# Counts of six expert searches from two tiles of tokens a matmul, with left sides of 128 columns

## The chip, the cores and the metric

One core of one Trainium2 chip runs the whole kernel as one program. The metric is the device time of one execution in microseconds (us); the time before is the median of three runs. The engines have the names of the profile: PE (TensorE's matmuls), PEld (its weight loads), DVE (VectorE), ACT (ScalarE), POOL (GpSimd) and SP (which issues most DMAs).

## The reference, cut to what matters

Three stages follow one another: attention over pooled keys and values, a layer of eight experts with a greedy assignment of tokens, and a two-layer MLP.

```python
def reference(**kwargs):
    attn_out = _attn_ref(**attn_kwargs)            # (8, 8, 576, 64)
    x = ascontiguousarray(attn_out.transpose(0, 2, 1, 3)).reshape(4608, 512)
    x = _moe_ref(x=x, **moe_kwargs)
    return _moe2_ref(x=x, **moe2_kwargs)           # h = x @ w_in; (h - tanh(h)) @ w_out

def _moe_ref(x, w_gate, w1, w2):                   # N = 4608 tokens, E = 8, F = 1024
    cap = N // E
    logits = x @ w_gate
    order = np.argsort(-logits.flatten())
    for idx in order:                              # largest logit first, over all tokens and experts
        tok, e = (int(idx) // E, int(idx) % E)
        if assigned[tok] >= 0 or counts[e] >= cap:
            continue
        assigned[tok] = e
        counts[e] += 1
    for e in range(E):
        mask = assigned == e
        h = np.maximum(x[mask] @ w1[e], 0.0)
        out[mask] = h @ w2[e]
```

An expert takes a token until it has 576 of them; then it is closed, and the tokens left over go to their next best open expert.

## The kernel before, in words

Tokens stand in 36 tiles of 128 (`NT = 36`), a token a partition. The greedy loop is replaced by a search: for the experts in the order in which they fill up (k = 0 to 7), the kernel finds the logit at which the next expert reaches 576 tokens (`fast_search` for k = 0, `search` for k = 1 to 6; k = 7 takes the rest without a search), closes that expert (`fill`), turns its tokens into a list of rows (`route_rows`) and gathers them (`gather`).

A search of k = 1 to 6 has two parts of three steps. In a step, DVE compares the key of each token with 40 to 42 thresholds and writes the ones and zeros as `at` [128, 36, n], n being the number of thresholds. `count` then adds over the tokens: for each tile j a matmul has `self.ohb[:, j, :]` on the left (128 tokens by 8, a one at the token's best expert) and `at[:, j, :]` on the right, and all 36 add up in `p2` [8, n] in PSUM: for each expert, how many of its tokens lie at or above each threshold. DVE compares `p2` with what each expert still lacks (`ok`, in a tile named `pass`, so it stands as `pass` in the profile), one matmul with ones (`pass,ones` in the profile) adds this over the experts for all partitions, and DVE makes the next threshold from it (`jm`). So a step is a chain: at on DVE, the count on PE, pass on DVE, a matmul on PE, jm on DVE. For k = 1 `at` and the count go in three pieces of 8, 12 and 16 tiles; for k = 2 to 6 DVE writes all 36 tiles in one instruction and the 36 matmuls are one unit for the planner (line 662; the matmuls that the planner places one by one stand on line 131). The search of k = 0 has six steps with 17 or 19 thresholds and three pieces.

`route_rows` builds two matrices of ones and zeros for each tile, `oa` (40 columns, the left side) and `ob` (32 columns), and adds `oa.T @ ob` over the 36 tiles in a PSUM tile `pp` named `tr`; `sp` and five matmuls with `sel5` (`sp,sel` in the profile) spread it.

An expert's products are 384 matmuls with 128 by 128 on the left and 288 columns on the right, in fp32r, split into high and low parts (`mm<-parts` and `m<-parts` in the profile).

The order on each engine is not written out by hand. `Plan` records every operation with an estimated cost, and `placed` puts the operations one after another, the most urgent first, into the earliest gap on their engine, where a reader on PE also gets a margin after its inputs: 0 for the routing of k = 1, 0.2 us for k = 2, 0.8 us for k from 3. The routing of expert k has an urgency so that it runs beside the products of experts k - 2 and k - 1. Each engine then executes its list in order.

The names and lines that matter: `count` (657), `fast_search` (681), `search` (762), `route_rows` (926), `Recorder` (131, the line on which every operation placed one by one is shown).

Of the kernel before, what the change touches and what calls it, by code (L numbers as in the profile page):

```python
# [9 lines left out]
F32 = mybir.dt.float32  # L10
F32R = mybir.dt.float32r
BF = mybir.dt.bfloat16
# [3 lines left out]
AF = mybir.ActivationFunctionType  # L16
OP = mybir.AluOpType
# [7 lines left out]
NT = N // 128  # L25
# [9 lines left out]
RADIX = 41  # L35
# [244 lines left out]
class Kernel:  # L280
# [25 lines left out]
    def route_consts(self, tp):  # L306
# [46 lines left out]
        nc.vector.tensor_scalar(t("w8c", [128, 1], F32), pef, -1.0, 8.0, op0=OP.mult, op1=OP.add)  # L353

        for nm, shape, dt in (("pass", [128, 18], F16), (f"pass{RADIX - 1}", [128, RADIX], F16),
                              (f"pass{RADIX}", [128, RADIX + 1], F16), ("dl", [128, 8], F16), ("sp", [128, 32], BF)):
            nc.vector.memset(t(nm, shape, dt), 0.0)
            if nm[:4] == "pass":
                nc.vector.memset(c[nm][:8, shape[1] - 1:], 1.0)
# [247 lines left out]
    def best(self, js=slice(0, NT), first=False):  # L607
# [19 lines left out]
        V.tensor_tensor(sg, mi, sg, op=OP.bitwise_xor)  # L627
        self.ohb = rp.tile([128, NT, 8], BF, name="ohb")
        V.tensor_tensor(self.ohb[:, js], oh, bc(mw), op=OP.is_equal)
# [26 lines left out]

    def count(self, out, at, js, whole=False):

        if whole:
            def products():  # L660
                for j in js:
                    last = self.nc.tensor.matmul(out, self.ohb[:, j, :], at[:, j, :], start=j == 0, stop=j == NT - 1)  # L662
                return last

            self.plan.call("tensor", products, [self.ohb, at], [out], 0.026 * len(js) + 0.18)
            return
        for j in js:
            self.plan.tensor.matmul(out, self.ohb[:, j, :], at[:, j, :], start=j == 0, stop=j == NT - 1)

# [14 lines left out]
    def fast_search(self, hl):  # L684
# [15 lines left out]
        for i in range(6):  # L700
# [4 lines left out]
            for a, b in ((0, 8), (8, 20), (20, NT)):  # L705
                x = v[:, a:b, None].to_broadcast([128, b - a, n])
                y = c["th"][:, i, None, :n].to_broadcast([128, b - a, n])
                if t is None:
                    V.tensor_tensor(at[:, a:b], x, y, op=OP.is_ge)
                else:  # L710
                    V.scalar_tensor_tensor(at[:, a:b], x, t, y, op0=OP.subtract, op1=OP.is_ge)
                self.count(p2, at, range(a, b))
            if i == 0:
# [43 lines left out]
    def search(self, k, hl):  # L757
# [5 lines left out]
        for part in range(2):  # L763
            t = None
            for i in range(3):
# [5 lines left out]
                p2, p3 = bank[:8, :n], bank[:, 128:128 + n + 1]  # L771
                for a, b in ((0, 8), (8, 20), (20, NT)) if k == 1 else ((0, NT),):
                    x = v[:, a:b, None].to_broadcast([128, b - a, n])
                    y = th[:, None, :].to_broadcast([128, b - a, n])
                    if t is None:
                        V.tensor_tensor(at[:, a:b], x, y, op=OP.is_ge)
                    else:
                        V.scalar_tensor_tensor(at[:, a:b], x, t, y, op0=OP.subtract, op1=OP.is_ge)
                    self.count(p2, at, range(a, b), k > 1)
                if part and i == 0:  # L780
# [9 lines left out]
                if t is None:  # L790
                    ok = ok[:, :n]
                    inc = inc[:, :n]
                    p3 = p3[:, :n]
                V.tensor_scalar(ok[:8, :n], p2, lack, None, op0=OP.is_ge)
                nc.tensor.matmul(p3, c["ones"], ok, start=True, stop=True)
# [5 lines left out]
            y1, z1 = [rp.tile([8, RADIX], F32, name=nm) for nm in ("y1", "z1")]  # L801
            nc.scalar.activation(z1, p2, AF.Copy)
            nc.scalar.activation(y1, p3[:8, :n], AF.Copy)
# [5 lines left out]
        jn = rp.tile([8, RADIX + 1], F32, name="j8")  # L809
        V.tensor_scalar(jn, p2, lack, 0.0, op0=OP.is_ge, op1=OP.add, accum_out=ne)  # L810
        V.tensor_scalar(c["dl"][:8], c["blk"][:8], ne, None, op0=OP.mult)
        p4 = bank[:, 256:264]
        nc.tensor.matmul(p4, c["ones"], c["dl"], start=True, stop=True)
        y2 = rp.tile([8, RADIX + 1], F32, name="z2")
        nc.scalar.activation(y2, p2, AF.Copy)
        nm = rp.tile([128, 1], F32, name="nm")
# [110 lines left out]
    def route_rows(self, k, g):  # L927
# [11 lines left out]
        V.tensor_copy(gb, g2)  # L939
        oa = rp.tile([128, NT, 40], BF, name="oa")  # L940
        ob = rp.tile([128, 3, NT, 16], BF, name="ob")
        for j in range(0, NT, 12):
# [6 lines left out]
            else:  # L949
                nc.scalar.activation(ob[:, 1, js], ob[:, 2, js], AF.Copy, scale=c["pcol"])  # L950
            V.tensor_tensor(oa[:, js], bc(gb[:, 0, js], 40),
                            c["iota40"][:, None, :].to_broadcast([128, 12, 40]), op=OP.is_equal)
        pp = self.rps.tile([40, 32], F32, name="tr")
        for j in range(NT):
            nc.tensor.matmul(pp, oa[:, j, :], ob[:, 0:2, j, :], start=j == 0, stop=j == NT - 1)
        sp = c["sp"]
        V.tensor_copy(sp[:40], pp)
        pi = self.rps.tile([128, 5, 32], F32, name="tr")
# [93 lines left out]
    def products(self, nc, out, terms, first=True, last=True):  # L1052

        n = len(terms)
        for i, (wh, wl, xh, xl) in enumerate(terms):
            nc.tensor.matmul(out, wh, xh, start=first and i == 0, stop=False)
            nc.tensor.matmul(out, wh, xl, start=False, stop=False)
            nc.tensor.matmul(out, wl, xh, start=False, stop=last and i == n - 1)
# [411 lines left out]
```

## Time and profile before

| | us |
|---|---|
| median of three runs | 1487.55 (1486.27 to 1489.66) |
| profiled execution, its own time | 1487.64 |
| span of its core | 1485.9 |
| PE busy | 1441.4 (97%) |
| PEld busy | 1271.1 (86%) |
| DVE busy | 1190.2 (80%) |
| ACT busy | 809.2 (54%) |
| POOL busy | 318.2 (21%) |
| PE's share of the chain that ended last | 85% |

The execution has four stretches: attention until about 156 us, the routing of k = 0 until about 186 us, the experts with the routing of k = 1 to 7 beside their products until about 700 us, and the second MLP until the end. In the views, a row of the timeline gives the start of the first instruction of a group and the time until the end of its last; matmuls are pipelined, so a matmul's own duration (180 ns for one of the count) overlaps the next one's, and what a matmul costs its engine is read from start to start. A row's last bracket is the time the engine sat idle before it and what ended that.

### The profile page before, as it was taken

What the parts mean: (1) busy time and instruction counts of PE and PEld (TensorE: products, weight loads), DVE (VectorE), ACT (ScalarE), POOL (GpSimd) and SP (SyncE); (2) the same over time, 40 slices, a digit from 0 to 9 for tenths busy, and PEclk for the clock granted to TensorE, in tenths of its full rate; (3) what the DMA queues carried; (4) which work ended last, traced back from release to release, by engine and by line L of the source; (5) the groups of instructions that cost most, each with busy time, mean ns of one, the idle gap of its engine ahead of it and who ended that gap; (6) DMA issues with size and microseconds to landing.
All of it is one profiled execution on the core that took longest, in us unless ns stands there. A gap on an engine that the chain in (4) does not pass through costs nothing.

```text
span 1485.9 us, 25650 instructions
## 1 busy us (share of the span) xinstructions
PE 1441.4 (97%) x9763; PEld 1271.1 (86%) x9764; DVE 1190.2 (80%) x2506; ACT 809.2 (54%) x1463; POOL 318.2 (21%) x292
## 2 busy tenths in 40 slices
PE   8999599999999999999999999999999999999997
PEld 6999488999999999999788888888888888888885
DVE  8778878787899976875998787878878788787874
ACT  5444123335455576866665565655656565665653
POOL 5874101202224155553401010000101000010101
PEclk9999699999999999999999999999999999999999
DMA  9941124324525367665200010100001010000000
GB/s 385 373 175 74 52 67 137 108 67 144 185 86 189 102 190 252 232 212 159 71 30 29 1 57 1 37 21 29 29 1 57 1 36 22 29 29 1 29 1 28
DMA packets 98315, 138.51 MB, mean 93 GB/s; under 512 B 6928, under 2 KB 70416, under 8 KB 95504
## 3 DMA queue, kind: packets, MB, share of 16 engines
q1 hardware_dynamic: 87632, 108.04, 21.8%
q0 software_dynamic: 5952, 19.40, 3.7%
q10 hardware_dynamic: 4608, 9.44, 1.7%
q8 instruction: 76, 1.25, 0.4%
q14 instruction: 47, 0.39, 0.1%
HBM read 103.30 MB, written 33.55 MB: 92 GB/s over the span
## 4 chain that ended last, share of the span: by engine, by line
PE 85%; DVE 9%; issue 2%; DMA 2%; ACT 1%; POOL 1%; POOLq 0%; ACTq 0%; DVEq 0%; SPq 0%
PE mm L131 40%; PE m L131 19%; PE tr L131 8%; PE rt L131 7%; PE av L131 4%; PE sc L131 3%; PE pt L131 2%; DVE parts L131 2%; PE rt L662 2%; DVE g L131 2%; DVE ca L131 1%; DVE gl L131 1%; DMA xg<-xd,ix 1%; DVE oa L131 1%; DVE ob L131 0%
## 5 line engine op out<-in xcount | busy, mean ns | idle before, releaser
L131 PE MATMUL mm<-parts 128*128 128x288 f32 x2112 | 306.5, 300 | 2.0 <-DVE parts L131 2.0
L131 PEld LDWEIGHTS mm<-parts 128*128 128x128 f32 x2112 | 287.4, 189 | 4.8 <-DVE parts L131 2.2
L131 PE MATMUL mm<-parts,gh 128*128 128x512 f32 x792 | 244.0, 389 | 0.0
L131 DVE SCALAR_TENSOR_TENSOR g<-s,g 128x512 f32<-128x512 f32 x288 | 205.6, 714 | 2.8
L131 ACT ACTIVATE s<-u,pb 128x512 f32<-128x512 f32 x288 | 192.3, 724 | 0.0
L131 PEld LDWEIGHTS mm<-parts,gh 128*128 128x128 f32 x792 | 148.7, 188 | 30.8
L1319 POOL DMA_INDIRECT out<-y,ix x18 | 20.4, 1133 | 658.1 <-ACT y L131 637.4
L131 PE MATMUL mm<-parts,gl 128*128 128x512 f32 x396 | 154.4, 390 | 0.8 <-DVE gl L131 0.8
L131 PE MATMUL m<-parts 128*128 128x288 f32 x960 | 143.7, 302 | 0.1
L131 PE MATMUL m<-yh,parts 128*128 128x512 f32 x432 | 141.9, 389 | 0.0
L131 ACT ACTIVATE parts<-wr 128x512 fp32r<-128x512 f32 x148 | 90.9, 626 | 86.8 <-DMA wr<-w 32.7
L131 DVE TENSOR_TENSOR parts<-wr,parts 128x512 fp32r<-128x512 f32 x128 | 101.0, 804 | 42.1 <-ACT parts L131 41.7
L131 PEld LDWEIGHTS m<-parts 128*128 128x128 f32 x960 | 133.0, 191 | 1.1 <-DVE parts L131 0.2
L131 ACT ACTIVATE gh<-g 128x512 fp32r<-128x512 f32 x144 | 91.2, 633 | 74.0 <-DVE g L131 51.4
L131 DVE TENSOR_TENSOR gl<-g,gh 128x512 fp32r<-128x512 f32 x144 | 106.5, 740 | 21.1 <-ACT gh L131 21.1
L131 DVE COPY_PREDICATED g<-m,t 128x512 f32<-128x512 uint32 x144 | 109.5, 761 | 5.0
L131 ACT ACTIVATE u<-m 128x512 f32<-128x512 f32 x72 | 42.9, 596 | 116.2 <-PE m L131 116.2
L131 PEld LDWEIGHTS m<-yh,parts 128*128 128x128 f32 x432 | 81.1, 188 | 16.8
L131 DVE TENSOR_TENSOR g<-m,u 128x512 f32<-128x512 f32 x72 | 49.6, 688 | 54.5 <-ACT t L131 53.4
L131 PEld LDWEIGHTS mm<-parts,gl 128*128 128x128 f32 x396 | 74.4, 188 | 17.1 <-DVE gl L131 1.7
L131 PE MATMUL m<-yl,parts 128*128 128x512 f32 x216 | 84.1, 389 | 0.0
L131 PE MATMUL tr<-yh,parts 128*128 128x512 f32 x216 | 70.9, 389 | 0.0
(273 smaller groups left out, 2866.0 us busy)
## 6 DMA issues: line engine op xcount, KB each, us to landing
wr<-w SPq DMA_DIRECT2D x64, 512.0 KB, 4.2
xd<-x SPq DMA_DIRECT2D x36, 256.0 KB, 2.4
yd<-y ACTq DMA_DIRECT2D x32, 288.0 KB, 3.3
raw<-wi SPq DMA_DIRECT2D x32, 256.0 KB, 4.7
raw<-wo SPq DMA_DIRECT2D x32, 256.0 KB, 3.6
kr<-k SPq DMA_DIRECT2D x7, 1152.0 KB, 8.5
qT<-q SPq DMA_DIRECT2D x7, 1152.0 KB, 9.2
vr<-v SPq DMA_DIRECT2D x7, 1152.0 KB, 11.4
```

What stands on the lines that cost most here:

```text
L131: op = self.call(engine, lambda: f(*args, **kw), ins, outs, cost, delay)
L662: last = self.nc.tensor.matmul(out, self.ohb[:, j, :], at[:, j, :], start=j == 0, stop=j == NT - 1)
L1319: st = nc.gpsimd.indirect_dma_start(out=self.io["out"], in_=o, in_offset=None, out_offset=bass.IndirectOffsetOnAxis(ap=at, axis=0))
```

## The change

Three things change in `count` and its surroundings.

- **Left sides of 128 columns.** `ohb` and `oa` get zeroed padding behind the last tile, so that 128 columns from the first column of tile j can always be read. For k = 0 the left side of the count is then 16 tiles of `ohb` (128 columns) and the result has 128 rows, of which the first 8 are used; `route_rows` reads 128 columns of `oa` and uses the first 40 rows.
- **Two tiles a matmul for k = 1 to 6.** `count_pairs` puts `ohb[:, j:j+16]` on the left and the columns of tiles j and j + 4 of `at` on the right (2n columns). Rows 0 to 7 of the first n columns then hold the count of tile j, rows 32 to 39 of the other n columns that of tile j + 4. Sixteen matmuls do 32 tiles, and tiles 0 to 3 go alone with n columns: 20 matmuls in place of 36. The pieces of k = 1 become 12, 16 and 8 tiles.
- **The halves are added on the way.** ACT copies rows 32 to 39 of the second half to SBUF with the sign turned (`less`), and DVE's `pass` becomes `p2 - lack >= less`. The copies `z1` and `y2` on ACT become subtractions on DVE.

The planner gets a cost of its own for the 20 matmuls, and its extra cost for small left sides no longer applies to counts and rows.

```diff
@@ route_consts
+        for nm, n, m in (("ohb", 15, 8), ("oa", 3, 40)):
+            c[nm] = self.rp.tile([128, NT + n, m], BF, name=nm)
+            nc.vector.memset(c[nm][:, NT:], 0.0)
@@ best
-        self.ohb = rp.tile([128, NT, 8], BF, name="ohb")
+        self.ohb = self.c["ohb"]
@@ count, for k = 0
-            self.plan.tensor.matmul(out, self.ohb[:, j, :], at[:, j, :], start=j == 0, stop=j == NT - 1)
+        m = out.shape[0] // 8
+            self.plan.tensor.matmul(out, self.ohb[:, j:j + m].rearrange("p t e -> p (t e)"), at[:, j, :], start=j == 0, stop=j == NT - 1)
@@ new, for k = 1 to 6
+    def count_pairs(self, bank, at, a, b, n, whole=False):
+        T = self.nc.tensor if whole else self.plan.tensor
+        def products():
+            for j in [*range(4, 8), *range(4), *range(8, NT)]:
+                if not a <= j < b:
+                    continue
+                left = self.ohb[:, j:j + 16].rearrange("p t e -> p (t e)")
+                if j < 4:
+                    last = T.matmul(bank[:, :n], left, at[:, j, :], start=False, stop=False)
+                elif j % 8 >= 4:
+                    last = T.matmul(bank[:, :2 * n].rearrange("p (t m) -> p t m", t=2), left, at[:, j:j + 5:4],
+                                    start=j == 4, stop=j == NT - 5)
+            return last
+        if whole:
+            self.plan.call("tensor", products, [self.ohb, at], [bank[:, :2 * n]], 16 * (n / 1200 + 0.003) + 0.104)
+        else:
+            products()
@@ fast_search
-                self.count(p2, at, range(a, b))
+                self.count(bank[:, :n], at, range(a, b))
@@ search
-                for a, b in ((0, 8), (8, 20), (20, NT)) if k == 1 else ((0, NT),):
+                for a, b in ((0, 12), (12, 28), (28, NT)) if k == 1 else ((0, NT),):
-                    self.count(p2, at, range(a, b), k > 1)
+                    self.count_pairs(bank, at, a, b, n, k > 1)
+                less = rp.tile([8, RADIX + 1], F32, name="less", bufs=2)[:, :n]
+                nc.scalar.activation(less, bank[32:40, n:2 * n], AF.Copy, scale=-1.0)
-                V.tensor_scalar(ok[:8, :n], p2, lack, None, op0=OP.is_ge)
+                V.scalar_tensor_tensor(ok[:8, :n], p2, lack, less, op0=OP.subtract, op1=OP.is_ge)
-            nc.scalar.activation(z1, p2, AF.Copy)
+            V.tensor_tensor(z1, p2, less, op=OP.subtract)
-        V.tensor_scalar(jn, p2, lack, 0.0, op0=OP.is_ge, op1=OP.add, accum_out=ne)
+        V.scalar_tensor_tensor(jn, p2, lack, less, op0=OP.subtract, op1=OP.is_ge, accum_out=ne)
-        nc.scalar.activation(y2, p2, AF.Copy)
+        V.tensor_tensor(y2, p2, less, op=OP.subtract)
@@ route_rows
-        oa = rp.tile([128, NT, 40], BF, name="oa")
+        oa = self.c["oa"][:, :NT]
-        pp = self.rps.tile([40, 32], F32, name="tr")
+        pp = self.rps.tile([128, 32], F32, name="tr")
+        left = self.c["oa"].rearrange("p j a -> p (j a)")
-            nc.tensor.matmul(pp, oa[:, j, :], ob[:, 0:2, j, :], start=j == 0, stop=j == NT - 1)
+            nc.tensor.matmul(pp, left[:, 40 * j:40 * j + 128], ob[:, 0:2, j, :], start=j == 0, stop=j == NT - 1)
```

Because the planner sees other costs, it places the work anew. On PE, in the first step of the search of k = 2, the end of the count, the products of expert 0 (`m<-parts`) that stand between it and the matmul of `pass`, and those that follow were before:

```order
L662 MATMUL rt_1641<-at_1640,ohb_226 8x40
L662 LDWEIGHTS ohb_226
L662 MATMUL rt_1641<-at_1640,ohb_226 8x40
L131 MATMUL m_0_1698<-parts 128x288 x5
L131 LDWEIGHTS ones
L131 MATMUL rt_1641<-pass_162,ones 128x40
L131 MATMUL m_0_1698<-parts 128x288 x5
L131 MATMUL m_0_1670<-parts 128x288 x13
```

and are now (80 columns are the two tiles):

```order
L684 MATMUL rt_1644<-at_1643,ohb_161 128x80
L684 LDWEIGHTS ohb_161
L684 MATMUL rt_1644<-at_1643,ohb_161 128x80
L131 MATMUL m_0_1702<-parts 128x288 x7
L131 LDWEIGHTS ones
L131 MATMUL rt_1644<-pass_164,ones 128x40
L131 MATMUL m_0_1702<-parts 128x288 x9
L131 MATMUL m_0_1672<-parts 128x288 x9
```

Seven products instead of five stand between the count and the matmul that needs its result; for k = 4 to 6 there are in most steps 12 instead of 10.

On PE in the third step of k = 1, the end of the last piece of the count before:

```order
L131 MATMUL rt_1641<-at_1640,ohb_226 8x41
L131 MATMUL mm_1681<-parts 128x288 x4
L131 LDWEIGHTS ones
L131 MATMUL rt_1641<-pass_163,ones 128x42
L131 MATMUL mm_1681<-parts 128x288 x10
```

and now:

```order
L131 MATMUL rt_1644<-at_1643,ohb_161 128x82
L131 MATMUL mm_1683<-parts 128x288 x6
L131 LDWEIGHTS ones
L131 MATMUL rt_1644<-pass_165,ones 128x42
L131 MATMUL mm_1683<-parts 128x288 x8
L131 MATMUL mm_1682<-parts 128x288 x3
```

Four products between count and pass have become six. The five later steps of k = 1 had three runs of count matmuls each, 15 in all; now they have 13, since in two of the steps the last two pieces stand together.

On DVE in the first step of k = 2 the new order is (hi and lo parts of weights are `parts<-wr`):

```order
L131 TENSOR_TENSOR at_1643<-hl_228,thr 128x1440
L131 TENSOR_TENSOR parts<-wr_1701,parts 128x512 x2
L131 SCALAR_TENSOR_TENSOR pass_164<-rt_1644,lack,less_1685 8x40
L131 TENSOR_TENSOR parts<-wr_1700,parts 128x512
L131 SCALAR_TENSOR_TENSOR jm_1648,t_1_1688<-rt_1644,inc 128x40
```

`pass` now also waits for `less` of ACT; behind it in DVE's list stands one conversion of weights, then `jm`.

## Rows read from the trace of the kernel before

**Rows 1.** Busy time by stretch (start and end; length; each engine; clock; DMA)

```profile
156.00:186.00 30.00, 16.12 (x291) 11.30 (x293) 24.71 (x100) 3.56 (x7) 5.66 (x6) 0.54 0.16 48
...
196.00:218.00 22.00, 22.00 (x271) 18.89 (x270) 17.39 (x56) 5.61 (x13) 0.00 (x0) 1.00 0.12 37
...
300.00:400.00 100.00, 100.00 (x1093) 96.11 (x1093) 80.76 (x222) 43.72 (x84) 18.37 (x18) 1.00 0.36 114
400.00:500.00 100.00, 99.92 (x1090) 96.20 (x1090) 90.04 (x219) 59.73 (x113) 34.13 (x25) 1.00 0.42 136
```

**Rows 2.** Timeline, k = 2, first step (PE; DVE's pass): start, time until end, group

```profile
241.69 1.22 PE L131 MATMUL m<-parts 128*128 128x288 f32 x8
242.84 1.07 PE L662 MATMUL rt<-at,ohb 128*8 128x40 bf16 x36
243.84 0.93 PE L131 MATMUL m<-parts 128*128 128x288 f32 x5
...
243.95 0.25 DVE L131 TENSOR_SCALAR pass<-rt,lack 8x40 f16<-8x40 f32 x1 [0.37 <-PE rt L662]
...
244.61 0.19 PE L131 MATMUL rt<-pass,ones 128*128 128x40 f16 x1
244.65 2.64 PE L131 MATMUL m<-parts 128*128 128x288 f32 x18
247.21 1.07 PE L662 MATMUL rt<-at,ohb 128*8 128x40 bf16 x36
```

**Rows 3.** The chain that ended last: start, time, 48 products in a row

```profile
338.58 6.36 PE mm L131 x48
```

**Rows 4.** Groups by form on PE and PEld: count, busy us, mean ns, idle before

```profile
L662 PEld LDWEIGHTS <-ohb 128*8 128x8 bf16 x1080 | 28.6, 83 | 5.0 <-issue 4.4 <-DVE e L131 0.5
...
L131 PEld LDWEIGHTS <-sel 128*128 128x128 bf16 x40 | 1.8, 97 | 4.2 <-issue 3.5
...
L131 PE MATMUL tr<-ob,oa 128*40 128x32 bf16 x288 | 9.5, 179 | 4.8 <-POOL ob L131 3.9 <-DVE oa L131 0.8
```

**Rows 5.** PE's timeline around the rows of k = 3

```profile
330.24 1.46 PE L131 MATMUL mm<-parts 128*128 128x288 f32 x9
331.56 0.28 PE L131 MATMUL tr<-sp,sel 128*128 128x32 bf16 x5
331.68 2.51 PE L131 MATMUL mm<-parts 128*128 128x288 f32 x17
```

**Rows 6.** PE's timeline: first matmuls of the program in two windows, and attention's last count

```profile
4.94 2.11 PE L552 MATMUL av<-junk 128*128 128x512 bf16 x9
...
5.16 1.46 PE L552 MATMUL av<-junk 128*128 128x512 bf16 x6
...
151.23 2.14 PE L131 MATMUL pt<-at,ohb 128*8 128x127 bf16 x34
```

**Rows 7.** PE's timeline, k = 1, third step

```profile
198.72 0.36 PE L131 MATMUL rt<-at,ohb 128*8 128x41 bf16 x8
...
199.33 0.46 PE L131 MATMUL rt<-at,ohb 128*8 128x41 bf16 x12
...
200.32 0.57 PE L131 MATMUL rt<-at,ohb 128*8 128x41 bf16 x16
```

**Rows 8.** Groups by form on ACT and DVE, 238 to 510 us

```profile
L131 ACT ACTIVATE parts<-mm 128x576 fp32r<-128x576 f32 x20 | 12.9, 647 | 11.4 <-PE mm L131 11.4
...
L131 ACT ACTIVATE z<-rt 8x41 f32<-8x41 f32 x5 | 1.0, 195 | 2.4 <-DVE pass L131 2.4
...
L131 DVE TENSOR_SCALAR pass<-rt,lack 8x40 f16<-8x40 f32 x20 | 4.8, 242 | 2.0 <-PE rt L662 1.9
```

**Rows 9.** Timeline of k = 0, second step: DVE and PE

```profile
159.03 1.11 DVE L131 SCALAR_TENSOR_TENSOR at<-w,ft,th 128x136 bf16<-128x136 f32 x3
159.44 1.31 PE L131 MATMUL rt<-at,ohb 128*8 128x17 bf16 x36 [0.75 <-DVE at L131]
```

**Rows 10.** Waits of PE, 185 to 705 us: total, times, longest

```profile
PE tr L131 <- DVE sp L131: 2.4, 2, 2.3
```

More of the change, by code (lines that the diff above doesn't have):

```diff
@@ L655, in first_best, with count @@
             P.gpsimd.tensor_scalar(at, at, 0.0, None, op0=OP.is_ge)
-    def count(self, out, at, js, whole=False):
-        if whole:
[L660 to L667, printed above, removed]
-            self.plan.tensor.matmul(out, self.ohb[:, j, :], at[:, j, :], start=j == 0, stop=j == NT - 1)
+    def count(self, out, at, js):
+        m = out.shape[0] // 8
+        for j in js:
+            self.plan.tensor.matmul(out, self.ohb[:, j:j + m].rearrange("p t e -> p (t e)"), at[:, j, :], start=j == 0, stop=j == NT - 1)
[12 more added lines that the diff above has]
+            return last
+        if whole:
+            self.plan.call("tensor", products, [self.ohb, at], [bank[:, :2 * n]], 16 * (n / 1200 + 0.003) + 0.104)
+        else:
+            products()
     def first_part(self, p2, p3, pool):
@@ L952, in route_rows @@
                             c["iota40"][:, None, :].to_broadcast([128, 12, 40]), op=OP.is_equal)
-        pp = self.rps.tile([40, 32], F32, name="tr")
+        pp = self.rps.tile([128, 32], F32, name="tr")
+        left = self.c["oa"].rearrange("p j a -> p (j a)")
         for j in range(NT):
-            nc.tensor.matmul(pp, oa[:, j, :], ob[:, 0:2, j, :], start=j == 0, stop=j == NT - 1)
+            nc.tensor.matmul(pp, left[:, 40 * j:40 * j + 128], ob[:, 0:2, j, :], start=j == 0, stop=j == NT - 1)
         sp = c["sp"]
-        V.tensor_copy(sp[:40], pp)
+        V.tensor_copy(sp[:40], pp[:40])
         pi = self.rps.tile([128, 5, 32], F32, name="tr")
```

## The prediction, made before the changed kernel ran

> **What bounds the kernel now.** I read the stretches first, then PE's timeline inside them, because a share of the whole span says nothing about a change that sits in one stage. From 196 us on, PE is busy for the whole of a stretch: 22.00 of 22, 100.00 of 100 and 99.92 of 100 us, while DVE has 17.39, 80.76 and 90.04 and ACT at most 59.73 [rows 1]. So the searches of k = 1 to 6, which lie in these stretches, run beside the products of experts, and what they take from PE lengthens the kernel one for one. Only the routing of k = 0 (156 to 186 us) is a chain with an idle PE, 16.12 of 30 us, at a mean clock of 0.54 [rows 1]. The waits of PE between 185 and 705 us come to little, the longest kind 2.4 us [rows 10]. Therefore the question is how many microseconds of PE a count costs, before and after.
>
> **A count before, k = 2 to 6.** The undisturbed price of a product is 6.36 us / 48 = 0.1325 us [rows 3]. In the first step of k = 2 the eight products before the count should take 8 x 0.1325 = 1.06 us, but the count starts 242.84 - 241.69 = 1.15 us after them: entering it costs 0.09. The count takes 243.84 - 242.84 = 1.00. The five products behind it take 244.61 - 243.84 = 0.77 where 0.66 is their price: 0.11 more [rows 2]. Together 1.20 us of PE for one count. There are 1080 weight loads of this form, so 30 such counts [rows 4].
>
> **A count after.** Twenty matmuls, sixteen with 80 to 84 columns and four with 40 to 42.
> - A wide one: of the bf16 matmuls of 512 columns at the program's start, with 128 columns on the left, nine take 2.11 us and six 1.46; three more take 0.65, so 0.217 each, 3 ns above their columns at 2.4 a ns. The bf16 count of 127 columns at the end of attention has 34 in 2.14 us, with about 0.2 for the last, 0.058 a matmul, 5 ns above its columns [rows 6]. So 80 columns cost 0.036 to 0.040; I take 0.037, nearer to the first, because that one has 128 columns on the left as well.
> - A narrow one: the matmuls `sp,sel` have 128 bf16 columns on the left and 32 on the right; five of them take 331.68 - 331.56 = 0.12 us, 0.025 each [rows 5]. So a left side of 128 columns can be loaded every 25 ns, and its load lasts 97 ns against 83 for 8 columns [rows 4].
> - Entry: before `sp,sel`, nine products take 1.32 us; their price is 1.19 and the 0.11 behind a group with a narrow left side belongs to its exit, so 0.02 is left: no entry cost. Exit: between the `pass` matmul, which has 128 columns on the left, and the next count, 18 products take 2.56 us; their price is 2.385 and the entry of that count 0.09, so 0.085 is the exit [rows 2, 5]. The last wide matmul adds about 0.01.
>
> Sum: 16 x 0.037 + 4 x 0.025 + 0.10 = 0.79 us. A count saves 1.20 - 0.79 = 0.41, thirty of them **12.2 us**.
>
> **The counts of k = 1.** Its three pieces stand apart among expert 0's products [rows 7], and each pays entry and exit: 36 take 1.07 us with 0.18 for the last [rows 2, 4], so start to start is 0.0254, a count 36 x 0.0254 = 0.91 us, and every run of it costs 0.28 on top (0.09, 0.11, and the 0.085 by which the 1.00 is longer). Fifteen runs in five steps: 5 x 0.91 + 15 x 0.28 = 8.8. After: 5 x 0.69 + 13 x 0.10 = 4.75. That saves **4.0 us**. The first step lies among transposes that wait for gathered rows, where PE has idle time; I count nothing there.
>
> **The rows.** `ob,oa` keeps its 36 matmuls at 0.025 each, as `sp,sel` shows for 128 columns; the entry of 0.09 and most of the other excess goes, 0.28 - 0.10 = 0.18 for each of k = 2 to 7. For k = 1 two groups become one, about 0.4. Of the 288 matmuls of the form [rows 4], those of k = 0 wait for DVE and POOL and gain nothing. Sum **1.5 us**.
>
> **The search of k = 0** has its 36 matmuls in 1.31 us behind three pieces of `at` that take DVE 1.11 [rows 9]; the last start to start is 25 ns there too, so wider left sides give nothing as long as they load at that pace: 0, with a bound of 0.1 us a step either way. The two memsets lie in attention, where DVE's list has gaps; they are small (120 columns).
>
> **What the change adds.** ACT gets `less` in each of 36 steps, 0.195 us by `z<-rt`, a copy of the same shape [rows 8]. It is in the chain: PE's last matmul (0.18), hand-over (0.04: the count ended at 242.84 + 1.07 = 243.91, `pass` on DVE started at 243.95 [rows 2]), `less` 0.20, hand-over 0.04, `pass` 0.24 [rows 8], and 0.05 to PE: 0.75 us. `z1` and `y2` move from ACT to DVE at about 0.2 us each, off PE. What hides the longer chain is the products in front of the `pass` matmul: six for k = 1, 0.04 + 0.22 + 5 x 0.1325 = 0.92 us after the last start; seven for k = 2, 1.05; twelve later, 1.7. So the cover is 0.17 us for k = 1 and 0.3 for k = 2, and an ACT instruction in front (up to 0.647, [rows 8]) breaks it. PE then stalls with all products behind it, and DVE, waiting for `less`, holds its conversions. I charge 12 steps x 0.13 = **1.6 us**, between 0 (ACT free, as in most of k = 1) and 12 x 0.6 = 7.
>
> Sum: 12.2 + 4.0 + 1.5 - 1.6 = 16.1 us. The profiled execution took 1487.64 us, its span 1485.9 and 1.7 around it; it lies 0.1 above the median. So **1471.5 us**, and by the bounds of the wide matmul (+1.7, -0.6) and of the stalls (+5.4, -1.6), and with the waits of [rows 10] falling otherwise in the new order (2 either way), 1467 to 1478.
>
> **A rule against it.** The rows show 25 ns from start to start with 128 columns on the left. The Trainium skill (TensorE: Matmul & The Clock Gate, sections "LDWEIGHTS (loading the stationary operand)" and "Weight-path perf modes — Fast Weight Load (FWL) and DoubleRow") gives a load the number of its columns / 1.2 ns, 107 ns for 128, and the fast load about twice that speed as measured. By an estimate from this page, 53 ns a matmul, a count of 20 would take 1.06 + 0.10 us and save almost nothing, and the rows would become slower. The trace differs: its `sp,sel` matmuls would need 0.27 us, and took 0.12.
>
> **The rivals.**
> - *DVE becomes the bound.* It has 90.04 of 100 us between 400 and 500 [rows 1]. PE gives up about 4 us there, and DVE gets 0.4 us more an expert: 90.5 of 96. For it: DVE stands in line order, and PE waited for `sp` already [rows 10]. Against it: conversions of the second MLP's weights, which nobody awaits there, are part of the 90. If k = 4 to 6 lose what they gain, 18 x 0.41 = 7.4: 1479.
> - *Nothing is gained*, since the freed time is waited away in several places: 1487.6. Against it: from 196 to 500 us PE has no idle time that could show such a limit.
> - *`less` comes late everywhere.* If ACT's list holds `less` back by a uniform L, PE stalls 6 x (L - 0.17) + 6 x (L - 0.3) + 24 x (L - 0.95). At L = 1.25, two ACT instructions, that is 6.5 + 5.7 + 7.2 = 19, more than the 17.7 gained: from there on it is slower. At 1.5 us it gives 8 + 7.2 + 13.2 = 28, so 1498. Against it: ACT is busy 44 to 60% of the stretches where most steps lie [rows 1].
> - *Loads of the new left sides don't hide.* A fp32r product behind a short matmul starts its successor 0.085 later than usual, so its own load of 128 four-byte columns holds PE for about 0.12 us; half of that for two-byte columns is 0.06. Then a count costs 1.3 (30 x 0.1 = 3 lost), the counts of k = 1 gain 1.5, each `ob,oa` loses 36 x 0.035 - 0.18 = 1.1 (7.5 in all): 1498 with the stalls. The rule of the Trainium skill quoted above (TensorE: Matmul & The Clock Gate, section on the fast weight load) points the same way. Against it: `sp,sel`.
>
> **How the numbers follow.** Forecast 0.70; DVE 0.16; nothing gained 0.05; `less` late 0.05; loads 0.04. The predicted time is the forecast's. The forecast with its bounds and the DVE case leave out under 2 in 10 with 1466 to 1482. A measurement of this kernel can tell about 0.2% (3 us) from no change; faster gets the first two cases, 0.86, same 0.05, slower 0.09.
>
> **What would show it.** The forms of the count: 600 in place of 1080 on the line of whole counts, start to start 0.036 to 0.040 for the wide ones; products before a count without the 0.09. A group of five products behind a count should show 0.085 in place of 0.11. The products should start as early as the sum says: the second MLP about 16 us sooner. Wrong if PE shows new waits for `pass`, if DVE's share between 400 and 500 us reaches 96, if the wide matmuls start 0.05 us apart, or if the clock, 1.00 in the stretches from 196 us on [rows 1], falls there.

## The result and the profile after

The changed kernel takes 1474.41 us (median of four, 1472.5 to 1476.58); the kernel before, run beside it, 1488.21 (1486.27 to 1489.66). The ratio is 0.9908, 95% interval 0.9896 to 0.992: 13.8 us faster. The forecast was 1471.5, 16 us faster; the time lies in its range of 1466 to 1482 and on the forecast's side. The profiled execution took 1474.56 us, its span 1472.8.

The first step of k = 2 on PE, which answers to [rows 2] (start, time until the end, group):

```profile
241.07 0.70 PE L131 MATMUL mm<-parts 128*128 128x288 f32 x4
241.61 0.32 PE L684 MATMUL rt<-at,ohb 128*128 128x80 bf16 x4
241.76 0.26 PE L681 MATMUL rt<-at,ohb 128*128 128x40 bf16 x4
241.87 0.59 PE L684 MATMUL rt<-at,ohb 128*128 128x80 bf16 x12
242.29 1.16 PE L131 MATMUL m<-parts 128*128 128x288 f32 x7
243.30 0.19 PE L131 MATMUL rt<-pass,ones 128*128 128x40 f16 x1
```

The four products before the count take 241.61 - 241.07 = 0.54 us, 0.01 over 4 x 0.1325: the entry of 0.09 is gone. The count takes 242.29 - 241.61 = 0.68. The seven products behind it take 1.01 where 0.93 is their price: 0.08. Together 0.77 where the prediction has 0.79, and 1.20 before. From start to start the wide matmuls take 0.035 to 0.039 us (medians for 80 to 84 columns) and the narrow ones 0.025. The groups by form count 600 matmuls in whole counts, in place of 1080 [rows 4]:

```profile
L684 PEld LDWEIGHTS <-ohb 128*128 128x128 bf16 x480 | 20.5, 98 | 2.6 <-issue 0.4
L684 PE MATMUL rt<-at,ohb 128*128 128x80 bf16 x320 | 16.9, 201 | 0.4 <-DVE at L131 0.4
L681 PEld LDWEIGHTS <-ohb 128*128 128x128 bf16 x120 | 5.6, 97 | 0.0
```

A load of 98 ns stands every 25 to 39 ns, and PE starts its matmuls at that pace: the loads hide. The stretches (start and end; length; busy time of PE, PEld, DVE, ACT, POOL; clock; DMA), against [rows 1]:

```profile
156.00:186.00 30.00, 17.08 (x300) 12.09 (x298) 24.37 (x99) 4.12 (x9) 6.48 (x7) 0.54 0.17 55
196.00:218.00 22.00, 22.00 (x219) 20.75 (x217) 18.73 (x65) 6.85 (x17) 0.00 (x0) 0.96 0.16 49
300.00:400.00 100.00, 100.00 (x949) 97.69 (x949) 83.91 (x228) 45.30 (x90) 19.69 (x20) 1.00 0.43 137
400.00:500.00 100.00, 98.58 (x950) 95.90 (x949) 91.83 (x249) 60.95 (x121) 31.65 (x23) 1.00 0.42 134
```

PE, busy for 99.92 us between 400 and 500 before, has 1.4 us of holes there now, and DVE has come closer to it. The clock of 0.96 between 196 and 218 belongs to this execution: it is 0.55 until 198 us and 1.00 from there, and in the second run of the same kernel (r0, below) the stretch has 1.00 and the lower level comes behind it, 0.57 between 218 and 226. PE's waits between 185 and 695 us (total, times, longest), against [rows 10]:

```profile
PE mm L131 <- DMA xg<-xd,ix: 3.0, 3, 2.0
PE tr L131 <- DVE oa L131: 2.5, 4, 1.1
PE m L131 <- DVE parts L131: 2.0, 2, 1.5
PE mm L131 <- DVE parts L131: 2.0, 1, 2.0
PE tr L131 <- DVE sp L131: 1.4, 1, 1.4
PE tr L131 <- ACT xg L131: 1.3, 2, 0.8
PE tr L131 <- DMA xg<-xd,ix: 1.3, 3, 0.5
PE rt L131 <- DVE pass L131: 1.1, 2, 0.7
PE rt L684 <- DVE at L131: 0.4, 1, 0.4
```

They sum to 15.0 us; before, the waits of this stretch sum to 9.5.

**Where the 13 us went.** I laid the PE instructions of each trace from 192.2 us (all products of experts but one come later) to the last product end to end, from start to start, and sorted the distances: the matmuls of counts; what products beside short matmuls take over 0.1325 us, up to 0.13 us each (entry and exit); `ob,oa`; what products take more while the granted clock is at the lower of its two levels (1.2 GHz); and everything longer, as waits. The rest is about the same in all kernels, 426 to 429 us. In us:

| | 192.2 to last product | counts | entry, exit | rows | lower clock | waits |
|---|---|---|---|---|---|---|
| before | 503.2 | 35.7 | 16.4 | 7.1 | 4.2 | 12.3 |
| the change | 488.8 | 24.3 | 12.2 | 6.6 | 2.0 | 16.4 |
| the change, run again (r0) | 487.9 | 23.9 | 12.2 | 6.6 | 3.9 | 15.7 |

Matmul work fell by 11.4 + 4.2 + 0.5 = 16.1 us. Waits rose by 4.1, in the second run by 3.4. The clock gave 2.2, but the second run of the same kernel only 0.3, so that belongs to the execution and not to the change. The second MLP, from the last product to the last matmul, is 1.3 us longer (779.3 to 780.6); this too is the execution's, for in the second run it is 779.5. So 16.1 + 2.2 - 4.1 - 1.3 = 12.9, of the 13.1 us by which the span is shorter.

### The profile page after: what moved, and what is told of

The parts are those of the page before. It is cut to its first block, busy times and chain, and to the rows that moved or that the text cites. A ratio compares the mean times of both kernels' runs of the same rounds, so it can differ in the third digit from the quotient of the medians.

```text
span 1472.8 us, 24523 instructions
## 1 busy us (share of the span) xinstructions
PE 1423.2 (97%) x9187; PEld 1258.4 (85%) x9188; DVE 1186.2 (81%) x2520; ACT 813.5 (55%) x1487; POOL 313.7 (21%) x292
## 4 chain that ended last, share of the span: by engine, by line
PE 79%; DVE 12%; DMA 3%; issue 2%; ACT 1%; POOL 1%; SPq 0%; ACTq 0%; POOLq 0%; DVEq 0%
PE mm L131 37%; PE m L131 18%; PE tr L131 7%; PE rt L131 7%; PE av L131 4%; PE sc L131 3%; DVE parts L131 2%; PE pt L131 2%; DVE g L131 2%; DVE ca L131 1%; PE rt L684 1%; DMA raw<-wo 1%; DVE oa L131 1%; DVE gl L131 1%; DMA xg<-xd,ix 1%
## 5 line engine op out<-in xcount | busy, mean ns | idle before, releaser
L131 DVE TENSOR_TENSOR parts<-wr,parts 128x512 fp32r<-128x512 f32 x128 | 97.5, 778 | 28.0 <-ACT parts L131 27.7
L131 ACT ACTIVATE u<-m 128x512 f32<-128x512 f32 x72 | 42.8, 595 | 115.7 <-PE m L131 115.7
```

What stands on the lines that cost most here:

```text
L131: op = self.call(engine, lambda: f(*args, **kw), ins, outs, cost, delay)
```

## The experiments

The first two runs take the change apart. After them the question was not whether PE is relieved, but why 4 us come back as waits, and what they wait for. Theories: (1) the added link `less` (an ACT copy inside each step) lengthens the chain at-count-less-pass-jm; (2) DVE has no time left, so whatever PE gives up is waited away behind DVE; later a third came: (3) the order in which the planner lays out DVE and ACT decides.

**Wide left sides alone (e1).** The kernel before with 128 columns on the left: 36 matmuls of one tile each, no pairs, no `less`. The planner is told 1.04 us for a count in place of 1.12, and `route_rows` has its wide left side. Against the kernel before:

```diff
-                    last = self.nc.tensor.matmul(out, self.ohb[:, j, :], at[:, j, :], start=j == 0, stop=j == NT - 1)
+                    left = self.ohb[:, j:j + m].rearrange("p t e -> p (t e)")
+                    last = self.nc.tensor.matmul(out, left, at[:, j, :], start=j == 0, stop=j == NT - 1)
...
-            self.plan.call("tensor", products, [self.ohb, at], [out], 0.026 * len(js) + 0.18)
+            self.plan.call("tensor", products, [self.ohb, at], [out], 0.026 * len(js) + 0.104)
```

> The kernel before with left sides of 128 columns alone (counts of all k and the rows), still 36 matmuls a count, no second half and no `less`. Theory (a narrow left side costs PE about 0.18 us at entry and exit of every run of matmuls, and nothing inside): 30 counts x 0.18 + 15 runs of k = 1 x 0.18 + rows 1.5 = 9.6 us less than before, about 1478.5, start to start inside a count still 0.025. Rival (the gain of the change is the smaller number of matmuls alone): within 2 us of before. Rival (wide loads don't hide): slower than before.

Measured: 1479.59 us against 1489.64, ratio 0.9936 (0.9923 to 0.995), 10.05 us faster, close to the 9.6 expected. PE's timeline in the same step:

```profile
240.12 0.70 PE L131 MATMUL mm<-parts 128*128 128x288 f32 x4
240.66 1.08 PE L668 MATMUL rt<-at,ohb 128*128 128x40 bf16 x36
241.58 0.91 PE L131 MATMUL m<-parts 128*128 128x288 f32 x5
242.33 0.19 PE L131 MATMUL rt<-pass,ones 128*128 128x40 f16 x1
```

No entry (0.54 for four), 0.92 for 36 matmuls, 0.09 of exit: 1.02 us together, so the width of the left side alone is worth 0.18 us a count. So 10 of the 13.8 us come without any pairing; 7.8 of them are matmul work by the account at the end of this section, and waits don't rise (11.4 us). The pairs take another 8.2 us of counts off PE (32.5 to 24.3) and bring only about 4.

**Pairs with a narrow left side (e2).** The change with 40 columns on the left; the planner is told 0.18 us more for a count.

```diff
-                left = self.ohb[:, j:j + 16].rearrange("p t e -> p (t e)")
+                left = self.ohb[:, j:j + 5].rearrange("p t e -> p (t e)")
```

> The change, but the left side of a pair has 40 columns (5 tiles of `ohb`) instead of 128, so 20 matmuls and `less` stay and only the width goes. Theory: the wide matmuls still start 0.036 to 0.040 apart, and every run has its 0.28 of entry and exit again: 30 x 0.18 + 13 x 0.18 = 7.7 us slower than the change, about 1482. Rival (the gain of the change is the smaller number of matmuls alone): as the change, 1474.4.

Measured: 1484.72 us, ratio 0.9968 (0.9956 to 0.998): 4.9 us faster than before, some 9 slower than the change by the ratios, where 7.7 was expected. PE:

```profile
243.93 0.70 PE L131 MATMUL mm<-parts 128*128 128x288 f32 x4
244.56 0.32 PE L684 MATMUL rt<-at,ohb 128*40 128x80 bf16 x4
244.71 0.26 PE L681 MATMUL rt<-at,ohb 128*40 128x40 bf16 x4
244.82 0.59 PE L684 MATMUL rt<-at,ohb 128*40 128x80 bf16 x12
245.34 1.19 PE L131 MATMUL m<-parts 128*128 128x288 f32 x7
```

The entry of 0.10 is back (0.63 for four products), the exit is 0.10, and the last matmul of the count takes 0.10 longer (0.78 in all). The three come with the narrow left side. By the account below, matmul work is 7.0 us above that of the change, and waits are 1.8 above.

**`less` on DVE (e3), `less` copied twice (e9).** e3 takes the hand-over to ACT out of the chain and puts the copy on DVE; e9 makes the ACT link twice as long.

```diff
-                nc.scalar.activation(less, bank[32:40, n:2 * n], AF.Copy, scale=-1.0)
+                V.tensor_scalar(less, bank[32:40, n:2 * n], -1.0, None, op0=OP.mult)
```

> The change with `less` made by DVE instead of ACT, so that ACT is out of the chain of a step. Theory (what was given back of the gain sits in waits of k = 0 and 1 for gathered rows, `oa` and low parts, not in `less`): within 2 us of the change, 1473 to 1476. Rival (ACT's list holds `less` back): 1.5 to 3 us faster than the change, and the waits of PE for `pass` (1.1 us in the trace of the change) gone.

```diff
+                half = rp.tile([8, RADIX + 1], F32, name="half", bufs=2)[:, :n]
+                nc.scalar.activation(half, bank[32:40, n:2 * n], AF.Copy, scale=-1.0)
+                nc.scalar.activation(less, half, AF.Copy)
```

> The change with `less` copied once more by ACT before `pass` reads it: the chain of each of 36 steps is about 0.3 us longer, DVE does what it did. Theory now (the planner sees the longer chain and puts more products in front of `pass`, and from k = 2 the cover holds): 0 to 2 us slower than the change, most of it in k = 1. Rival (the length of the chain sets the pace of the searches): 36 x 0.3 = 10 us slower.

Measured: e3 1483.08 us (ratio 0.995, 0.9936 to 0.9964), some 6 us slower than the change by the ratios, 9 by the medians; e9 1481.99 (0.9961, 0.9948 to 0.9975), 8 slower. For both I had expected at most 2 us more than the change, and for e9 named 10 as the other theory's: the first missed, and r13 below says why the second isn't proved by it. What had risen was PE's waits, from 16 to 23.6 and 22.7.

**More work on DVE (e8).** One more small DVE instruction a step, which reads the count's result.

```diff
+                V.tensor_scalar(rp.tile([8, RADIX + 1], F32, name="extra")[:, :n], p2, 1.0, None, op0=OP.mult)
```

> The change with one more instruction on DVE in five of the six steps of k = 1 to 6 (a copy of `p2` that nobody reads, about 0.24 us, behind `jm`, so off the chain): 30 x 0.24 = 7.2 us of DVE in all. Theory now (DVE has slack over the whole stretch; `less` on DVE cost 7 us because DVE's list was late at the steps themselves): 0 to 3 us slower than the change. Rival (DVE's load is the bound of the stretch): 6 to 8 us slower.

Measured: 1482.02 us (0.9956, 0.9943 to 0.997), 8.3 slower than the change. The 30 added instructions took 5.6 us (0.19 each, where 0.24 had been reckoned), less than what was lost. And 27 of the 30 stood right ahead of `pass` and not behind `jm`, so they lengthen the chain as well; the run doesn't tell (1) from (2).

**More margin in the plan (e4, e10).** The planner lets a reader on PE start that much after its inputs.

```diff
-            P.margin = 0.8 if k > 2 else 0.2 if k > 1 else 0.0
+            P.margin = 0.8 if k > 2 else 0.5 if k > 1 else 0.4 if k else 0.0
-            P.margin = 1.5 if k > 2 else 0.0
+            P.margin = 1.5 if k > 2 else 0.8
```

> The change with larger margins of the planner early on: 0.4 us for the routing of k = 1 (was 0), 0.5 for k = 2 (was 0.2), 0.8 for the gathers of k = 0 to 2 (was 0). Theory: the waits of PE for gathered rows, `oa` and low parts in k = 0 to 2 shrink from about 8 to 4 us or less and the kernel comes to 1470 to 1472. Rival (DVE is the bound, or the waits are lengths of chains that no order hides): 1473 to 1476, with the waits elsewhere.

```diff
-            P.margin = 0.8 if k > 2 else 0.2 if k > 1 else 0.0
+            P.margin = 1.6 if k > 2 else 0.8 if k > 1 else 0.4 if k else 0.0
-            P.margin = 1.5 if k > 2 else 0.0
+            P.margin = 2.0 if k > 2 else 0.8
```

> The change with still larger margins of the planner: 0.4 us for the routing of k = 1, 0.8 for k = 2, 1.6 for k from 3 (was 0.8), gathers 0.8 up to k = 2 and 2.0 later. Theory now (waits for `pass`, `sp` and gathered rows are DVE's list running behind the planner's times, so more distance hides them): 1 to 4 us faster than the change. Rival (the waits come from the amount of work and only move): within 1.5 us of the change.

Measured: e4 1474.17 us (0.9895, 0.988 to 0.991), the same as the change; e10 1490.4 (1.0011, 1.0002 to 1.0021), all of the gain lost where a gain of 1 to 4 us on the change was expected. In e4 the waits for `oa` shrank from 2.5 to 0.4 and those for low parts grew from 4.0 to 5.7. In e10:

```profile
PE m L131 <- DVE parts L131: 6.4, 3, 2.5
PE rt L131 <- ACT yh L131: 5.8, 1, 5.8
```

The searches end later: the last `at` of k = 6 starts at 512.1 us, in the change at 489.3. The waits are then for parts, and 5.8 us for `yh`, the high part of the second MLP's first inputs, so that stage starts late as well. My reading: the routing of an expert is about as long as the products beside it (some 60 us), so room given to its steps is taken from its end.

**The change again (r0).**

> The change itself once more, beside the next three on the same chip: 13 to 14.5 us under the kernel before.

Measured: 1473.7 us (0.9909, 0.9892 to 0.9926).

**The planner's number (r13, r15).** The variants that slowed down by about 8 us had one thing in common: the planner had laid everything out anew. So r13 is the change with nothing altered but the time that the planner is told for a count of k = 2 to 6, and r15 is the kernel before with the change's number:

```diff
-            self.plan.call("tensor", products, [self.ohb, at], [bank[:, :2 * n]], 16 * (n / 1200 + 0.003) + 0.104)
+            self.plan.call("tensor", products, [self.ohb, at], [bank[:, :2 * n]], 0.026 * NT + 0.18)
```

> The change with the planner told the old, longer duration for a count of experts 2 to 6, so that the same instructions are put in a somewhat other order. Both theories expect no more than 1.5 us either way; a larger shift would say that differences of a few us between the variants come from the planner's order as much as from what the variant changes.

```diff
-            self.plan.call("tensor", products, [self.ohb, at], [out], 0.026 * len(js) + 0.18)
+            self.plan.call("tensor", products, [self.ohb, at], [out], 16 * (at.shape[2] / 1200 + 0.003) + 0.104)
```

> The kernel before with one number altered: the planner is told 0.69 us for a whole count (the change's number) in place of 1.12, while its 36 matmuls still cost 1.20 us of TensorE. With the two runs of the change (0.69 told: 1474, 1.12 told: 1481.4) it completes a square of work and number. Theory 'the order that comes of a short number is good in itself': 5 to 8 us faster than before, 1480 to 1483.5. Theory 'the number must be near the true cost' (VectorE's list is laid out for a TensorE that is faster than it is): no gain or slower, 1487 to 1495, with VectorE waiting for counts in front of pass.

| | told 1.12 us | told 0.69 us |
|---|---|---|
| 36 narrow matmuls (true cost 1.20) | 1488.4 | 1489.3 (ratio 1.0, 0.999 to 1.001) |
| 20 wide matmuls (true cost 0.77) | 1481.4 (ratio 0.9953, 0.9939 to 0.9966) | 1474.4 |

The same instructions do the same work in another order, and 7 us of the 13.8 are gone: a miss for my "no more than 1.5". PE's own order hardly differs between 186 and 695 us (some 4309 of 4349 matmuls stand in the same sequence); on DVE it is some 951 of 1034 instructions, on ACT 434 of 543. A step of a search beside the products of expert 3 in the change (DVE and PE, timeline):

```profile
404.94 0.24 DVE L131 SCALAR_TENSOR_TENSOR pass<-rt,lack,less 8x40 f16<-8x40 f32 x1
405.10 0.67 DVE L131 TENSOR_TENSOR parts<-wr,parts 128x512 fp32r<-128x512 f32 x1
405.70 0.18 DVE L131 SCALAR_TENSOR_TENSOR jm<-rt,inc 128x40 f32<-128x40 f32 x1
...
408.49 0.30 PE L684 MATMUL rt<-at,ohb 128*128 128x80 bf16 x4
```

and the same step with the old number, with the GpSimd instruction that started just ahead of it:

```profile
408.56 1.28 POOL L131 TENSOR_TENSOR cm<-cm,ca 128x512 f32<-128x512 f32 x1 [2.90 <-DVE parts L131]
408.75 0.24 DVE L131 SCALAR_TENSOR_TENSOR pass<-rt,lack,less 8x40 f16<-8x40 f32 x1
408.91 1.48 DVE L131 TENSOR_TENSOR parts<-wr,parts 128x512 fp32r<-128x512 f32 x1
410.31 0.18 DVE L131 SCALAR_TENSOR_TENSOR jm<-rt,inc 128x40 f32<-128x40 f32 x1
...
413.11 0.30 PE L684 MATMUL rt<-at,ohb 128*128 128x80 bf16 x4 [0.75 <-DVE at L131]
```

From `pass` to `jm` it takes 0.76 us in the one and 1.56 in the other; in the second PE runs out of products before `at` is there and waits 0.75. In this step DVE's order is the same in both. What differs is the length of one instruction: the low part between them takes 0.67 and 1.48 us. The longest of the waits that are new in r13 is of the same kind (all engines, other rows left out):

```profile
358.26 1.29 POOL L131 TENSOR_TENSOR ca<-ca,cd 128x512 int32<-128x512 int32 x1 [19.56 <-DVE jm L131]
358.27 1.33 DVE L131 SCALAR_TENSOR_TENSOR w<-hl,t 128x36 f32<-128x36 f32 x1
...
359.63 1.29 POOL L131 TENSOR_TENSOR cm<-cm,ca 128x512 f32<-128x512 f32 x1
359.64 2.80 DVE L131 TENSOR_TENSOR at<-w,thr 128x1440 bf16<-128x1440 f32 x1
...
362.49 0.32 PE L684 MATMUL rt<-at,ohb 128*128 128x80 bf16 x4 [1.80 <-DVE at L131]
```

In the change the same two DVE instructions take 0.26 and 1.64 us, with no GpSimd instruction from 349 to 357 us, and PE doesn't wait. Over 238 to 640 us of the change, the 68 low parts of 128x512 with no GpSimd instruction beside them take 0.67 to 0.69 us, the 43 others 0.67 to 2.43. So a new order moves waits in two ways: by what stands in front of a step, and by which DVE instructions fall beside GpSimd's. No run tells how much of the 7 us is of either kind. In the kernel before, the short number doesn't help, because there the count is not done when DVE reaches `pass`. DVE's waits from 238 to 640 us in the kernel before, in r15 and in the change, one fence each:

```profile
DVE jm L131 <- PE rt L131: 11.1, 17, 1.4
DVE pass L131 <- PE rt L662: 1.9, 4, 0.7
```

```profile
DVE pass L131 <- PE rt L662: 8.6, 14, 1.5
DVE jm L131 <- PE rt L131: 7.7, 11, 1.3
```

```profile
DVE jm L131 <- PE rt L131: 6.0, 10, 1.2
DVE pass L131 <- ACT less L131: 3.4, 8, 0.8
```

The first and the third say what has turned: in the kernel before, DVE waits for PE 11.1 us in front of `jm`; after the change 6.0.

**Less DVE work (r12), and DVE work off the chain (r14).** r12 moves the low parts of a quarter of the weights of experts 1 to 5 to GpSimd (20 instructions). r14 adds an instruction that reads the step's threshold and is due late; it was meant to be one that nothing waits for.

```diff
-            P.vector.tensor_tensor(lo[:, r], raw[:, r], hi[:, r].bitcast(F32), op=OP.subtract)
+            E2 = P.gpsimd if h and i % 2 and 1 <= k <= 5 else P.vector
+            E2.tensor_tensor(lo[:, r], raw[:, r], hi[:, r].bitcast(F32), op=OP.subtract)
```

> The change with the low parts of a quarter of the weights of experts 1 to 5 computed on GpSimd instead of VectorE (some 20 instructions of 0.78 us, so 15 us less on VectorE during the searches). Theory 'VectorE's queue': the 3 us or so that the change lost behind VectorE come back: 1470 to 1472. Theory 'chain of the step': the chain has the same links; TensorE's waits for gathered rows, pass and oa stay: within 1 us of the change. A GpSimd instruction that is much slower than VectorE's would show as waits for low parts, and slower than the change by 2 to 5 us.

```diff
+                self.plan.urgency += 6.0
+                V.tensor_scalar(rp.tile([128, 128], F32, name="extra"), c["ahead"], t, None, op0=OP.add)
+                self.plan.urgency -= 6.0
```

> The change with one more VectorE instruction in each search step (128 columns, by the neighbouring rows about 0.2 us, some 30 of them: 6 us of VectorE), which reads the threshold that the step ends with, is due late, and which nothing waits for: it adds work to VectorE's queue but no link to the chain of a search step. Theory 'VectorE's queue': its spare time between 185 and 695 us is used up, so nearly all of the 6 us comes out as time: 5 to 8 us slower than the change, 1479 to 1482. Theory 'chain of the step': only links count, and the planner puts the instruction where VectorE waits: under 2 us slower, 1473.5 to 1476.

Measured: r12 1481.82 us (0.9952, 0.9939 to 0.9966), 7 slower than the change; r14 1506.31 (1.013, 1.0114 to 1.0145), 32 slower. Neither came out as a theory said. In r14 the added time is 30 x 0.281 = 8.4 us, and the loss is four times that:

```profile
PE rt L131 <- ACT yh L131: 9.2, 1, 9.2
PE mm L131 <- DVE parts L131: 8.2, 4, 3.4
PE m L131 <- DVE parts L131: 7.3, 4, 2.4
```

The low parts of weights come late, at four places each, and `yh` of the second MLP only after 9.2 us. But r14 isn't what it was meant to be. The tile of the threshold has two buffers (`bufs=2` in `search`), so `jm` of the third step writes the buffer that the added instruction of the first step reads, and the plan keeps a write behind the earlier reads. Through this the rest of the search depends, in the plan, on something that is due late, and is placed behind products that had been less urgent than the search. The fourth step of one search, DVE and PE:

```profile
441.89 1.65 DVE L131 TENSOR_TENSOR at<-w,thr 128x1440 bf16<-128x1440 f32 x1
...
446.19 12.91 PE L131 MATMUL mm<-parts 128*128 128x288 f32 x96
458.94 0.32 PE L684 MATMUL rt<-at,ohb 128*128 128x80 bf16 x4
```

Here `at` is ready at 443.5 us and its count starts at 458.94, with 96 products in a row ahead of it in PE's list. In the change the count of such a step starts 2.5 us after `at` does (417.13 and 419.65). For k = 3 to 6 this step takes 16 to 19 us from `at` to `pass` in r14 and 3.5 to 4.0 in the change, and a whole search, from the first `at` to the last, 46 to 49 us and 28 to 41. So r14 delays the search itself and says nothing about DVE work off the chain.

In r12 GpSimd took 1441 ns for a low part (the mean of its 40) that takes DVE 778 in the change, and PE's waits for `pass`, 1.1 in the change, were 3.0. The run didn't free DVE either: between 238 and 640 us DVE is busy for 337.66 us, against 338.61 in the change, though 20 low parts had gone. So neither run tests theory (2).

**All runs in the terms of the first table** (us):

| | counts, entry, exit, rows | lower clock | waits | median |
|---|---|---|---|---|
| before | 59.1 | 4.2 | 12.3 | 1488.2 |
| e1, wide alone | 51.3 | 4.0 | 11.4 | 1479.6 |
| e2, pairs narrow | 50.1 | 1.2 | 18.2 | 1484.7 |
| the change, r0 | 43.1, 42.6 | 2.0, 3.9 | 16.4, 15.7 | 1474.4, 1473.7 |
| e4, margins | 42.8 | 4.0 | 15.3 | 1474.2 |
| e3, e8, e9 | 42.3, 42.4, 41.6 | 5.2, 5.0, 3.8 | 23.6, 24.3, 22.7 | 1483.1, 1482.0, 1482.0 |
| r13, old number | 42.3 | 4.2 | 22.4 | 1481.4 |
| r12, low parts moved | 42.1 | 7.7 | 22.2 | 1481.8 |
| e10, more margins | 42.9 | 7.5 | 26.6 | 1490.4 |
| r14, DVE off the chain | 41.8 | 8.7 | 42.1 | 1506.3 |
| r15, before, new number | 58.9 | 4.1 | 15.7 | 1489.3 |

In all paired kernels with the wide left side the matmul work is 42 to 43 us; they differ in waits. The lower clock took most, 7.5 to 8.7 us, in three of the runs with long waits (r12, e10, r14), but e2 with waits of 18.2 has only 1.2 of it. The planner's order alone moves the waits by 6 us (the change against r13). That e3, e8, e9 and r12 lie within 2 us of r13 means that their edits can't be told from a re-planning: they show neither theory (1) nor (2). What their lists of waits have in common is what is late next once PE is relieved: the routing of the next expert, and the low parts that stand in DVE's list beside it. What stays open is which of the 4 us of new waits of the change come of `less`, which of the order and which of DVE instructions beside GpSimd's: no run held DVE's order fixed while `less` came and went. No version beat the change; e4 equals it.

## Why the prediction was right, and where it missed

- **A count, 1.20 to 0.79.** Right: 0.77 in the step shown. From 241 us to the last product, counts fell by 9.4 us and entry and exit (with those of the rows) by 3.0: 12.4 where 12.2 was predicted for the counts.
- **Counts of k = 1 and rows.** Predicted 4.0 and 1.5. Before 241 us counts fell by 2.0 and entry and exit by 1.2. The first table lists 0.6 us of k = 1 under waits that PE had in front of pieces of the count, and these fell away too: 3.8 around k = 1. `ob,oa` itself fell by 0.5 over the whole stretch. In all 16.7 of 17.7; the 1 us that is missing lies in these two terms.
- **k = 0: nothing.** Right. The first product starts 2.9 us earlier, but alone: the next stands at 192.29 us, behind gathered rows, as the first product does in the kernel before.
- **`less`, 1.6 us.** As a stall in front of the `pass` matmul it hardly exists: those waits went from 0.8 to 1.1 us. The cover of products held. DVE does wait for it: between 238 and 640 us 3.4 us in front of `pass` and 2.6 in front of `j`, the compare that ends a search, where before it waited 1.9 and 0.6 for the count. Whether some of PE's new waits come of that is not shown.
- **"With the waits falling otherwise in the new order, 2 either way."** This is the term that was too small. Waits rose by 4.1 us, for low parts, `oa` and gathered rows, and runs of nearly the same work in other orders had 6 to 10 more. I had read the 9.5 us of waits of the kernel before as something that stays. My reading now is that the routing chain is about as long as an expert's products, so that shorter products use up its slack; no run isolates this, and e1, with 7.8 us less matmul work, has no more waits than the kernel before. That the total still came within 3 us is in part luck: the 1.6 us charged for a stall that hardly came paid for part of these waits. The bounds as listed also add up to 1480.6 on the slow side, and not to 1478; the range of 1466 to 1482 holds both.
- **The rival "DVE becomes the bound".** Not as put: DVE reached 91.83 of 100 us, not 96, and k = 4 to 6 lost only some of their gain: the products beside them (769 to 1920 of 3072) take 182.2 us where they took 188.2, and 7.4 had been forecast. But my argument against it, that the conversions of the second MLP's weights are awaited by nobody, is wrong where the engine executes its list in order: `pass` and `jm` stand behind them. In the change, DVE waits 7.7 us between 300 and 640 us for the weights of the second MLP to land, with the steps of a search behind it, against 4.0 before.
- **The rival "loads don't hide", and with it the load rule of the Trainium skill** (TensorE: Matmul & The Clock Gate, sections "LDWEIGHTS (loading the stationary operand)" and "Weight-path perf modes — Fast Weight Load (FWL) and DoubleRow"). Read as the pace of matmuls, 53 ns by the prediction's estimate, the trace is against it: 25 ns from start to start with 128 columns of bf16 on the left, though one load lasts 98 ns.
- **A term that the prediction did not have:** the planner's number for a count, one line of the diff. Without it the same matmuls gain 7 us instead of 13.8 (r13); given to the kernel before alone, it gains nothing (r15).

## What to carry to other kernels

A matmul's left side that doesn't use all 128 columns can cost TensorE time at the borders of its group: here reading 128 columns in place of 8 or 40, with the results of the others unused and the same number of matmuls, gave 10 us. When a unit of work gets cheaper, tell the planner, and expect part of the gain only: here 4 of 16 us came back as waits, and with the old number 10. A variant of a planned kernel that comes out 7 us slower says nothing about the edit until a run with only the order altered has been set beside it. And before an added instruction is called free, look at what it reads: with two buffers, the second write after it has to wait for it, and a planner that thinks it may come late moves that write too (r14).

## What the runs showed of the hardware that I had not expected

- A narrow left side between 128-column products costs at both borders, and it is its width alone: 0.09 to 0.10 us at entry with 8 columns and with 40, 0.01 with 128; at the end 0.08 to 0.10 more in the group's last matmul (0.11 to 0.13 us to the next start, against 0.03). The 0.08 us behind a group remain for 128 columns too.
- bf16 matmuls with 128 by 128 on the left and 40 columns on the right start every 25 ns, with 80 to 84 every 35 to 39 ns, though a load lasts 98 ns and a matmul 181 to 201.
- Between 238 and 640 us of the change a VectorE low part of 128x512 took 0.67 to 0.69 us with no GpSimd instruction beside it, and up to 2.43 us beside one. Twenty low parts moved to GpSimd (r12) left VectorE's busy time there at 337.66 us, against 338.61.
- Around r14's wait of 9.2 us the granted clock fell to the lower of its two levels (0.51 between 688 and 698 us), and by the account r14 lost 8.7 us to that level, against 2.0 and 3.9 in the two executions of the change.
